# Gated linear attention with a SoLU layer: weight pieces fetched apart, part of a conversion moved between two groups of masks, constants made on GpSimd, and a finish moved ahead

## The chip, the cores and the metric

The kernel runs on one core of one Trainium2 chip. The metric is the device time in microseconds (us) of one execution, as the median of three runs. A core has five engines with a queue of instructions each: TensorE (PE; its weight loads are shown as PEld), VectorE (DVE), ScalarE (ACT), GpSimd (POOL) and SyncE (SP), which here issues most of the transfers. They wait for one another by semaphores. Sixteen DMA engines move data between the device memory and the core's own memory.

## The reference

Four batches, eight heads, 768 tokens, 48 values a head. A state per head decays by a gate and takes up the product of key and value; the query reads it. The result, as 3072 rows of 384, goes through a layer with the activation x*softmax(x), a layer norm with gains, and a second matrix.

```python
for t in range(S):
    state = alpha[:, :, t, :, None] * state + np.einsum('bhd,bhe->bhde', k[:, :, t], v[:, :, t])
    y[:, :, t] = np.einsum('bhd,bhde->bhe', q[:, :, t], state)
# x: y as (B*S, H*D)
h = x @ w_in                      # w_in 384 x 1024, float64
solu = h * softmax(h)
ln = (solu - mean(solu)) / np.sqrt(var(solu) + 1e-06) * g_ln
out = ln @ w_out                  # w_out 1024 x 384, float64
```

## The kernel before

The tokens are cut into six groups of 128 per batch. For each group the kernel turns the gates, keys and queries so that the values of a head lie on the partitions, runs scans over the tokens (`scan_back`, `scan_on`), multiplies keys and queries with them, makes the scores of all pairs of tokens in two halves of the heads (`scores`), cuts them to the triangle (`masked`, by a product with a mask of ones and zeros), and reads values and state (`read_values`, `read_state`) into `y`. The four batches' `y` are then the input of `up` for this group: eight pieces of 128 columns, each with an exponential on ScalarE, a product on VectorE and a square on ScalarE. `down` multiplies with the second matrix, one "chunk" of 128 tokens at a time, and `finish` scales the chunk and stores it. The attention of group g+1 is woven into `up` of group g by tables of steps.

The head of the kernel, with cuts:

```python
load_first(alpha, an, 0)
nc.scalar.dma_start(out=ident, in_=inline(np.eye(P), "ident_c"))
nc.scalar.dma_start(out=mask, in_=inline(np.triu(np.ones((P, P))), "mask_c"))
# ... parity and gains, also from the scalar queue
load_first(k, kn, 0)
load_first(q, qn, 0)
# ... memsets on GpSimd: vt, unit, aT, hT, seed, state
load_v_first(0)
fetch(0, 3, 2)          # weight pieces 0 and 1 together into slots 3 and 4
fetch(2, 1, 2)          # pieces 2 and 3
nc.vector.memset(ones, 1.0)
# ...
warm(16)                # 16 matmuls of ones, nothing uses them
turned(an, ends_of(an), t)      # transposes on TensorE, with ident
# ... scans, keys, queries
scores(0, 0)
scores(0, 1, t)
read_begin()
for b in (2, 3):        # two of the four first masks go over ScalarE and GpSimd
    s = sT[:, b, 0:NP]
    nc.scalar.copy(out=s, in_=masks[0][b])
    nc.gpsimd.tensor_tensor(out=s, in0=s, in1=mask[:, None, :].to_broadcast([P, NP, P]), op=ALU.mult)
masked(0, range(2))
masked(1)
bits(0)
read_values(0)
gains()
keys_back(0)
in_range(0)
bits(1)
in_range(1)
for f in range(FC):     # up of group 0
    up_mm(0, f)
    # ...
```

The weights are float64 and the kernel computes in float32. `fetch` brings the raw words, and `bits` makes float32 of them in five VectorE operations; it can be called by halves. A `fetch` of n pieces brings each of its (two or three) parts in one transfer for all n.

```python
def bits(i, part=None):
    lo, hi = raws[i][:, :, :, 0], raws[i][:, :, :, 1]
    if part != 1:
        # ... two operations: top
    if part != 0:
        # ... three operations: low, low, and the sum into w_in or w_out
```

The second stretch that the change touches, the start of `up` of group 1, with the attention of group 2:

```python
for i in range(3):
    scan_back(2, i)
keys_T(2)
keys(2)                 # products on GpSimd
load(k, kn, 3)
scan_on(2, 2)
scan_on(2, 0)
read_values(1)
alpha_over(2)
load(alpha, an, 3)
down(3, 1, slice(3, HF))
# ...
first = dict(
    head={3: "keys_back", 5: "masked0", 6: "masked1"},
    behind={0: "states v", 1: "lasts on1", 2: "firsts", 3: "apart", 5: "decay", 7: "alpha back"},
    tail={4: "scores0", 5: "scores1", 6: "begin read0 read1"},
    middle={7: "read2 read3 values"},
)
# ... for g in range(1, G + 1):
    after = B - 1 if g == 1 else None
    for s in range(FC):
        at("head", s)
        up(g, s)
        if after is not None:
            finish(after)
            after = None
        at("behind", s)
        # ... running sums, down, tail
```

`lasts` and `firsts` turn the queries on VectorE and multiply them on GpSimd, `apart` multiplies them with the parity on ScalarE, `states` adds to the state. `finish` of a chunk is four small VectorE operations (the last of them 128x384), one power on GpSimd (`r`), one scaling on ScalarE (`o_sb`) and a store.

Of the kernel before, what the change touches and what calls it, by code (L numbers as in the profile page):

```python
# [14 lines left out]
ALU = mybir.AluOpType  # L15
AX = mybir.AxisListType
P = 128
# [15 lines left out]
def fast_path(ctx, tc, q, k, v, alpha, moe_w_in, moe_w_out, moe_g_ln, out):  # L33
# [12 lines left out]
    nc = tc.nc  # L46
    B, H, S, D = q.shape
# [30 lines left out]
    ident = const.tile([P, P], FP, name="ident")  # L78
    mask = const.tile([P, P], FP, name="mask")
    ones = const.tile([P, P], FP, name="ones")  # L80
# [148 lines left out]
    def scan_on(g, i):  # L229
        part = slice(NP * i, NP * i + NP)  # L230
        if i == 2:

            nc.vector.reciprocal(out=seed[:, :, 0:1], in_=h4[:, :, 1:2])
            nc.scalar.copy(out=fend[:, g], in_=h4[:, :, 1])
        scan(aT[:, part], aT[:, part], seed[:, part], False)
# [53 lines left out]
    def masked(half, batches=range(B)):  # L289
        a = masks[half]  # L290
        for b in batches:
            nc.vector.tensor_tensor(  # L292
                out=sT[:, b, half * NP : half * NP + NP], in0=a[b], in1=mask[:, None, :].to_broadcast([P, NP, P]),
                op=ALU.mult,
            )
# [198 lines left out]
    def down(n, half, part=slice(0, HF)):  # L494
        g, b = divmod(n, B)
        d = st[n]
        if half == 0 and part.start == 0:
            d["o"] = ps_o.tile([P, 512], FP, tag="o", name="o")
        for f in range(half * HF + part.start, half * HF + part.stop):
            nc.tensor.matmul(  # L500
                d["o"][:, 0 : DM + 1], lhsT=u_of(g, f)[:, b * P : b * P + P], rhs=w_out[:, f], start=(f == 0),
                stop=(f == FC - 1), skip_group_check=True,
            )
# [7 lines left out]
    def finish(n):  # L511
        g, b = divmod(n, B)
        d = st[n]
        s, o = sums[:, n], d["o"][:, 0:DM]
        t0 = b * S + g * P
        if g == G - 1:
            o_sb = work.tile([P, DM], FP, name="o_sb")
            r = gr[g]["r"][:, b : b + 1]
            nc.scalar.activation(out=o_sb, in_=o, func=AF.Copy, scale=r)
            nc.scalar.dma_start(out=out[t0 : t0 + P, :], in_=o_sb)  # L520
            d.clear()
            return
        nc.vector.tensor_copy(out=s[:, 0:1], in_=d["o"][:, DM : DM + 1])
        t = small.tile([P, 1], FP, name="t")
        nc.vector.scalar_tensor_tensor(
            out=t, in0=s[:, 0:1], scalar=-1.0 / DFF, in1=s[:, 0:1], op0=ALU.mult, op1=ALU.mult
        )
        nc.vector.tensor_tensor(out=s[:, 3:4], in0=t, in1=gr[g]["s"][:, b : b + 1], op=ALU.add)  # L528
        if g == 0:

            if not d.get("moved"):
                o = work.tile([P, DM + 1], FP, name="o_mean")[:, 0:DM]
            nc.vector.scalar_tensor_tensor(
                out=o, in0=mean_sb, scalar=s[:, 0:1], in1=d["o"][:, 0:DM], op0=ALU.mult, op1=ALU.add
            )
        r = small.tile([P, 1], FP, name="r")
        nc.gpsimd.tensor_tensor(out=r, in0=s[:, 3:4], in1=mhalf, op=ALU.pow)  # L537
        o_sb = work.tile([P, DM], FP, name="o_sb")
        nc.scalar.activation(out=o_sb, in_=o, func=AF.Copy, scale=r)  # L539
        nc.sync.dma_start(out=out[t0 : t0 + P, :], in_=o_sb)  # L540
        d.clear()
# [16 lines left out]
    def fetch(i, slot, n=1):  # L558

        kind, f = pieces[i]  # L560
        w = n * F // (2 if kind else KC)
        raw = room[:, 1536 * slot : 1536 * (slot + n)].bitcast(U32).rearrange("p (c f w) -> p c f w", f=w, w=2)
        if kind:
            parts = [(slice(0, P), c, moe_w_out[(f + c) * P : (f + c + 1) * P, :]) for c in range(2)]
        else:
            parts = [(slice(0, P), c, moe_w_in[c * P : (c + 1) * P, f * P : f * P + w]) for c in range(KC)]
        for rows, c, src in parts:
            if float64:
                nc.sync.dma_start(out=raw[rows, c].rearrange("p f w -> p (f w)"), in_=src.bitcast(U32))
            else:  # L570
                dst = w_out[rows, f + c, 0:DM] if kind else w_in[rows, c, f * P : f * P + w]
                nc.sync.dma_start(out=dst, in_=src)
        for m in range(n):
            raws[i + m] = raw[:, :, w // n * m : w // n * (m + 1)]
# [14 lines left out]
    def bits(i, part=None):  # L589
        if not float64:  # L590
            return
        lo, hi = raws[i][:, :, :, 0], raws[i][:, :, :, 1]
        if part != 1:
            made[i] = [
                two.tile([P, F], FP, tag="two", name=x).rearrange("p (c f) -> p c f", c=hi.shape[1])
                for x in ("top", "low")
            ]
            top = made[i][0].bitcast(U32)
            nc.vector.tensor_scalar(
                out=top, in0=hi, scalar1=3, scalar2=0x3FFFFFF8, op0=ALU.logical_shift_left, op1=ALU.bitwise_and  # L600
            )
            nc.vector.scalar_tensor_tensor(
                out=top, in0=hi, scalar=0xC0000000, in1=top, op0=ALU.bitwise_and, op1=ALU.bitwise_or
            )
        if part != 0:
            top, low = made.pop(i)
            nc.vector.tensor_scalar(
                out=low.bitcast(U32), in0=top.bitcast(U32), scalar1=0xFF800000, scalar2=None, op0=ALU.bitwise_and
            )
            nc.vector.scalar_tensor_tensor(out=low, in0=lo, scalar=2.0**-52, in1=low, op0=ALU.mult, op1=ALU.mult)  # L610
            nc.vector.tensor_tensor(out=place(i), in0=low, in1=top, op=ALU.add)
# [34 lines left out]
    def inline(x, name):  # L646
        return nc.inline_tensor(np.ascontiguousarray(x, np.float32), name=name).ap()

    load_first(alpha, an, 0)
    nc.scalar.dma_start(out=ident, in_=inline(np.eye(P), "ident_c"))  # L650
    nc.scalar.dma_start(out=mask, in_=inline(np.triu(np.ones((P, P))), "mask_c"))
    odd = np.arange(P) // E1 % 2
    nc.scalar.dma_start(out=parity, in_=inline(np.stack([1 - odd, odd], 1), "parity_c"))
    nc.scalar.dma_start(out=g_rows, in_=moe_g_ln.rearrange("(c p) -> c p", p=P))
# [7 lines left out]
    nc.gpsimd.memset(seed, 0.0)  # L662
    nc.gpsimd.memset(state, 0.0)
    load_v_first(0)
    fetch(0, 3, 2)
    fetch(2, 1, 2)
    nc.vector.memset(ones, 1.0)
    nc.vector.memset(small_ones, 1.0 / 32)
    nc.vector.memset(mhalf, -0.5)
    nc.vector.memset(mone, -1.0)  # L670
# [26 lines left out]
    for i in (2, 0, 1):  # L697
        if i == 1:
# [3 lines left out]
            out=qe if i == 2 else qv[:, part], in0=t[i], in1=aT[:, part, 1:SW], op=ALU.mult  # L702
# [7 lines left out]
    for b in (2, 3):  # L710
        s = sT[:, b, 0:NP]
        nc.scalar.copy(out=s, in_=masks[0][b])
        nc.gpsimd.tensor_tensor(out=s, in0=s, in1=mask[:, None, :].to_broadcast([P, NP, P]), op=ALU.mult)
    masked(0, range(2))
    masked(1)
    bits(0)
    read_values(0)
    gains()
    keys_back(0)
# [94 lines left out]
    for i in range(3):  # L814
# [2 lines left out]
    keys(2)  # L817
    load(k, kn, 3)
    scan_on(2, 2)
    scan_on(2, 0)  # L820
    read_values(1)
    alpha_over(2)
    load(alpha, an, 3)
    down(3, 1, slice(3, HF))

# [5 lines left out]
    )  # L833
    first = dict(
        head={3: "keys_back", 5: "masked0", 6: "masked1"},
        behind={0: "states v", 1: "lasts on1", 2: "firsts", 3: "apart", 5: "decay", 7: "alpha back"},
        tail={4: "scores0", 5: "scores1", 6: "begin read0 read1"},
        middle={7: "read2 read3 values"},
    )
# [51 lines left out]
    for g in range(1, G + 1):  # L891
        rise, att = g < G, g + 1 < G
        plan = first if g == 1 else usual

        def at(where, s):
            for what in plan[where].get(s, "").split() if att else ():
                attend(g + 1, what)

        after = B - 1 if g == 1 else None
        if not rise:  # L900
            break
        for s in range(FC):
            at("head", s)
            if rise:
# [4 lines that stand above are left out]
            if s == 0 and g > 1:  # L909
                token_sums(g - 1)  # L910
            at("behind", s)
            for f in centres.get(s, ()) if g == 1 else ():
                centre(f)
            if rise and s:
                running(g, s)
            at("middle", s)
            if rise and s == FC - 1:
                todo.append((g * B, 0))
            step = todo.pop(0)
            if step:  # L920
                n, half = step
                down(n, half)
                if half:
                    after = n
            at("tail", s)
        if after is not None:
            finish(after)
        todo = [(n, half) for n in range(g * B, g * B + B) for half in range(2)][1:]
# [30 lines left out]
    else:  # L959
# [9 lines left out]
        out=bad, in0=all_ok[0:1, 0:1], scalar1=float(P * ends[-1]), scalar2=None, op0=ALU.is_lt  # L969
# [451 lines left out]
```

## Time and profile before

| what | value |
|---|---|
| median of 3 runs | 380.51 us (380.48 to 380.82) |
| span of the profiled execution | 378.7 us |
| mean granted TensorE clock | 0.997 |
| VectorE in 94 to 119 us | busy nearly without a gap |
| weight pieces 0 and 1 | first use by VectorE at 25.28 us, after 0.72 us of waiting |
| first matmul of `up` of group 0 | 29.97 us |
| first matmul of `up` of group 1 | 102.58 us |
| loads of identity and mask | 64 KB each, 1.9 and 3.4 us from issue to landing |

The profile is one execution. Its page gives busy times of the engines, the span in 40 slices (a digit is the busy share in tenths), the DMA queues, a chain of work that ended last, and groups of instructions. The trace behind it can be asked for the timeline of an engine: start, duration, engine, line of the kernel, operation, output and inputs, count; in square brackets the idle time of the engine ahead of it and what ended it. A line that stands for several instructions is merged. A duration on TensorE ends where its model puts the end. TensorE executes a float32 matmul as two passes, which the counts show (32 records for `warm(16)`). "issue" is time in which an engine waited for nothing that the profile shows.

### The profile page before, as it was taken

The page shows a single profiled execution, that of the slowest core. Times are in us where ns is not written, and L with a number is a line of the kernel's source. Part 1 is how long each engine was busy: PE and PEld are TensorE (multiplying, and loading weights), DVE is VectorE, ACT ScalarE, POOL GpSimd, SP SyncE. Part 2 cuts the span into 40 slices and gives each one's busy share as a digit, 9 for nine tenths or more (in the row PEclk, how much of TensorE's full clock was granted, in tenths as well). Part 3 has the DMA queues.
Part 4 walks back from the last instruction along what each step waited for, and adds up shares of the span by engine and source line. Part 5 has one row for each costly group of instructions (what it writes and reads, how often), then busy time and mean ns, then how long its engine had stood idle before and what let it go on. Part 6 is the DMA issues. An engine that isn't in the chain of part 4 may idle for free.

```text
span 378.7 us, 10523 instructions
## 1 busy us (share of the span) xinstructions
PE 365.5 (97%) x4659; PEld 219.2 (58%) x4659; DVE 244.1 (64%) x379; ACT 146.8 (39%) x263; POOL 129.4 (34%) x134
## 2 busy tenths in 40 slices
PE   8779999999998999999999999999999999999995
PEld 8675355567654565555575555675556675555552
DVE  1988879988997876874665874665865411455410
ACT  3628774493455152224451224451233131233111
POOL 5040000042148970662630671630672420333210
PEclk9999999999999999999999999999999999999998
DMA  9983989304097001960002940002300000000011
GB/s 187 190 309 100 223 273 159 85 0 128 24 215 141 4 5 31 182 144 21 23 25 39 205 112 23 23 24 46 62 0 23 24 23 2 22 21 21 23 44 49
DMA packets 65526, 30.78 MB, mean 81 GB/s; under 512 B 47032, under 2 KB 63680, under 8 KB 65472
## 3 DMA queue, kind: packets, MB, share of 16 engines
q1 hardware_dynamic: 64448, 29.10, 34.5%
q10 hardware_dynamic: 1024, 0.92, 0.7%
q8 instruction: 38, 0.62, 0.7%
q14 instruction: 16, 0.13, 0.1%
HBM read 25.30 MB, written 4.72 MB: 79 GB/s over the span
## 4 chain that ended last, share of the span: by engine, by line
PE 74%; DVE 11%; DMA 4%; ACT 4%; SPq 3%; issue 2%; ACTq 0%
PE o L500 30%; PE h L389 26%; PE y L315 8%; PE a L281 5%; DMA an<-in_alpha_dram 3%; SPq L153 2%; DVE hT L222 2%; DMA qn<-in_q_dram 2%; DVE sT L292 1%; PE kv L364 1%; PE tp L300 1%; DVE aT L197 1%; DVE room L404 1%; SPq L141 1%; ACT sq L214 1%
## 5 line engine op out<-in xcount | busy, mean ns | idle before, releaser
L500 PE MATMUL o<-w_out,room 128*128 128x385 f32 x384 | 133.8, 491 | 0.0
L389 PE MATMUL h<-x,w_in 128*128 128x512 f32 x288 | 132.4, 599 | 0.5 <-DVE room L404 0.4
L500 PEld LDWEIGHTS o<-w_out,room 128*128 128x128 f32 x384 | 71.2, 190 | 55.8 <-issue 13.1
L389 PEld LDWEIGHTS h<-x,w_in 128*128 128x128 f32 x288 | 52.8, 189 | 59.7 <-issue 48.2
L404 DVE TENSOR_TENSOR room<-h,e 128x512 f32<-128x512 f32 x40 | 27.6, 690 | 81.2 <-ACT e L403 81.1
L403 ACT ACTIVATE e<-h 128x512 f32<-128x512 f32 x40 | 23.9, 597 | 107.3 <-PE h L389 107.3
L420 POOL TENSOR_TENSOR p<-p,e 128x512 f32<-128x512 f32 x30 | 41.8, 1394 | 15.7 <-ACT e L403 15.6
L537 POOL TENSOR_TENSOR r<-sums,mhalf 128x1 f32<-128x1 f32 x20 | 14.9, 747 | 80.5 <-DVE sums L528 80.4
L405 ACT ACTIVATE u<-room 128x512 f32<-128x512 f32 x40 | 25.2, 631 | 38.4 <-DVE room L404 38.4
L292 DVE TENSOR_TENSOR sT<-a,mask 128x512 f32<-128x512 f32 x42 | 26.1, 682 | 8.3 <-PE a L281 8.2
L263 POOL TENSOR_TENSOR state<-state,hT 128x192 f32<-128x192 f32 x20 | 11.3, 582 | 53.4 <-DVE hT L222 53.4
L243 POOL TENSOR_TENSOR kT<-kT,hT 128x1024 f32<-128x1024 f32 (+1 forms) x8 | 14.2, 1796 | 42.2 <-DVE kT L197 42.2
L222 DVE TENSOR_TENSOR_SCAN hT<-aT,unit 128x516 f32<-128x516 f32 x18 | 23.2, 1355 | 7.5 <-ACT aT L683 7.4
L420 DVE TENSOR_TENSOR p<-p,u 128x512 f32<-128x512 f32 x30 | 22.8, 759 | 6.5 <-ACT u L405 6.5
L222 DVE TENSOR_TENSOR_SCAN aT<-aT,seed 128x516 f32<-128x516 f32 x18 | 26.6, 1508 | 0.2
L281 PEld LDWEIGHTS a<-qv,kT 32*128 32x128 f32 x704 | 21.8, 186 | 8.5 <-issue 2.4
L281 PE MATMUL a<-qv,kT 32*128 32x128 f32 x704 | 24.5, 278 | 1.7 <-POOL qv L254 0.8
L315 PE MATMUL y<-sT,vn 128*32 128x128 f32 x768 | 23.6, 274 | 2.6 <-issue 2.1
L315 PEld LDWEIGHTS y<-sT,vn 128*32 128x32 f32 x768 | 20.9, 110 | 4.8 <-issue 3.8
L214 ACT ACTIVATE sq<-an,mone 128x1536 uint8<-128x1536 f32 x12 | 18.9, 1574 | 0.2
L315 PE MATMUL y<-qv,state 32*32 32x128 f32 x960 | 16.7, 277 | 0.1
L539 ACT ACTIVATE o_sb<-o,r 128x384 f32<-128x384 f32 x16 | 9.3, 581 | 18.8 <-POOL r L537 18.8
(146 smaller groups left out, 373.0 us busy)
## 6 DMA issues: line engine op xcount, KB each, us to landing
an<-in_alpha_dram SPq DMA_DIRECT2D x20, 192.0 KB, 4.2
vn<-in_v_dram SPq DMA_DIRECT2D x10, 384.0 KB, 6.3
out_dram<-o_sb SPq DMA_DIRECT2D x20, 192.0 KB, 1.9
room<-in_moe_w_in_dram SPq DMA_DIRECT2D x6, 512.0 KB, 8.4
room<-in_moe_w_out_dram SPq DMA_DIRECT2D x8, 384.0 KB, 4.1
kn<-in_k_dram SPq DMA_DIRECT2D x16, 192.0 KB, 4.8
qn<-in_q_dram SPq DMA_DIRECT2D x16, 192.0 KB, 3.6
kn<-in_k_dram SPq DMA_DIRECT2D x4, 384.0 KB, 5.9
```

The lines of the kernel that those rows point to most:

```text
L214: nc.scalar.activation(out=sq, in_=x, func=AF.Relu, scale=sign, bias=mone, accum_out=over[:, g, i : i + 1])
L222: nc.vector.tensor_tensor_scan(out=o, data0=a, data1=s, initial=1.0, op0=ALU.mult, op1=ALU.add)
L281: nc.tensor.matmul(a[b][:, i], lhsT=kT[quarter(b), kb], rhs=qv[quarter(b), qb], start=kb == h, stop=kb != h, tile_position=(32 * b, 0), sk ...
L292: nc.vector.tensor_tensor(out=sT[:, b, half * NP : half * NP + NP], in0=a[b], in1=mask[:, None, :].to_broadcast([P, NP, P]), op=ALU.mult,)
L315: nc.tensor.matmul(y_bank(b)[quarter(r), a], lhsT=lhsT, rhs=rhs, start=(b, r) not in begun, stop=stop, tile_position=(row, 32 * r), skip_g ...
L389: nc.tensor.matmul(h, lhsT=w_in[:, a, f * P : (f + 1) * P], rhs=d["x"][:, a].rearrange("p b t -> p (b t)"), start=(a == 0), stop=(a == KC ...
L403: nc.scalar.activation(out=e, in_=h, func=AF.Exp)
L404: nc.vector.tensor_tensor(out=u, in0=h, in1=e, op=ALU.mult)
L405: nc.scalar.activation(out=u2, in_=u, func=AF.Square)
L420: eng.tensor_tensor(out=p, in0=d[0][i] if f == 1 else p, in1=d[f][i], op=ALU.add)
L500: nc.tensor.matmul(d["o"][:, 0 : DM + 1], lhsT=u_of(g, f)[:, b * P : b * P + P], rhs=w_out[:, f], start=(f == 0), stop=(f == FC - 1), skip ...
L537: nc.gpsimd.tensor_tensor(out=r, in0=s[:, 3:4], in1=mhalf, op=ALU.pow)
```

## The change

Four things change. Identity and mask are no longer loaded but made on GpSimd from a tile of ones, which is now set first. The first two weight pieces come by separate transfers, so that the first can be used before the second is there. The first two of the five operations that convert piece 0 stand between the masks of the first and of the second scores, so that VectorE has something to do while the second scores are made. And at the start of `up` of group 1 the finish of the fourth chunk stands ahead of the loop, no longer behind the first piece, while one scan moves from ahead of the loop to behind its second piece, and the turning of the queries' ends by one step.

```diff
     load_first(alpha, an, 0)
-    nc.scalar.dma_start(out=ident, in_=inline(np.eye(P), "ident_c"))
-    nc.scalar.dma_start(out=mask, in_=inline(np.triu(np.ones((P, P))), "mask_c"))
+    nc.vector.memset(ones, 1.0)
+    for x, op in ((ident, ALU.is_equal), (mask, ALU.is_ge)):
+        nc.gpsimd.affine_select(
+            out=x, in_=ones, pattern=[[1, P]], compare_op=op, fill=0.0, base=0, channel_multiplier=-1
+        )
@@
-    fetch(0, 3, 2)
+    fetch(0, 3)
+    fetch(1, 4)
     fetch(2, 1, 2)
-    nc.vector.memset(ones, 1.0)
@@
     masked(0, range(2))
+    bits(0, 0)
     masked(1)
-    bits(0)
+    bits(0, 1)
     read_values(0)
@@
     scan_on(2, 2)
-    scan_on(2, 0)
     read_values(1)
     alpha_over(2)
     load(alpha, an, 3)
     down(3, 1, slice(3, HF))
+    finish(3)
@@ first = dict(
-        behind={0: "states v", 1: "lasts on1", 2: "firsts", 3: "apart", 5: "decay", 7: "alpha back"},
+        behind={0: "states v", 1: "on0 on1", 2: "lasts firsts", 3: "apart", 5: "decay", 7: "alpha back"},
@@
-        after = B - 1 if g == 1 else None
+        after = None
```

## The prediction

> **What bounds the kernel now.** I read the page first, then the chain that ended last for the two stretches that the diff edits, then the timeline of each engine there, then the DMA queues by window. The page says that TensorE carries the kernel:
>
> ```profile
> PE 365.5 (97%) x4659; PEld 219.2 (58%) x4659; DVE 244.1 (64%) x379; ACT 146.8 (39%) x263; POOL 129.4 (34%) x134
> ...
> PE   8779999999998999999999999999999999999995
> ```
>
> Of 378.7 us, 13.2 are without a matmul. Only slices 1 to 3 (to 28.4 us) are visibly thin. So a change can gain only where TensorE waits: about 4.3 us in 8 to 30 us (by stages 4.54 busy of 6.70, 5.29 of 5.50, 7.89 of 9.80), and small pieces later. Everything that only moves other engines under a full TensorE is worth nothing.
>
> The head, from the chain in order of time (start, us, what):
>
> ```profile
> 8.09 6.59 DMA qn<-in_q_dram
> ...
> 16.71 0.69 DVE qe L701
> ...
> 22.10 0.68 DVE sT L292
> 22.78 0.04 issue
> 22.82 1.07 PE y L315 x23
> 23.89 1.49 issue
> 25.38 3.04 PE y L315 x101
> 28.42 0.15 PE tp_g L622
> 28.57 1.46 PE tp L300 x12
> 30.03 2.75 PE h L389 x6
> ```
>
> The reader is to see that the queries' arrival starts the path, that four masks by VectorE release the value reads `y`, and that these stand still for 1.49 us on nothing that a semaphore explains. From 30.03 the up-projection `h` runs almost without a gap.
>
> The second stretch, from the timelines of VectorE, ScalarE, GpSimd and TensorE (start, us, engine, line):
>
> ```profile
> 103.74 4.48 DVE L222 TENSOR_TENSOR_SCAN aT<-aT,seed 128x516 f32<-128x516 f32 x2
> 108.14 0.66 DVE L404 TENSOR_TENSOR room<-h,e 128x512 f32<-128x512 f32 x1
> ...
> 105.70 0.58 ACT L403 ACTIVATE e<-h 128x512 f32<-128x512 f32 x1
> ...
> 102.87 4.26 POOL L243 TENSOR_TENSOR kT<-kT,hT 128x1024 f32<-128x1024 f32 x2 [8.18 <-DVE kT L197]
> ...
> 119.57 0.50 PE L281 MATMUL a<-qv,kT 32*128 32x128 f32 x8 [0.76 <-POOL qv L254]
> 120.58 2.01 PE L281 MATMUL a<-qv,kT 32*128 32x128 f32 x56 [0.51 <-ACT qv L247]
> ```
>
> Here VectorE is dense from 94 to 119 us; TensorE pays 0.76 + 0.51 us before the scores of the third group. A second score group at 125.29 takes 3.44 us where its like takes 2.07, another 1.4 us behind the masks.
>
> [...] in 0 to 6 us queue q10 (identity, mask, parity, gains) took 9.3% of the 16 engines, 0.56 us, while q1 brought alpha and the keys. [...] three scans at 97.18 take 3.58 us (1.19 each), the two beside GpSimd's key products 2.24 each. [...] The trace has 38 packets of 0.62 MB, 16.3 KB each; one of them at 22.0 to 22.5 us, three us ahead of the end of the 1.49 us stop. That this packet is the awaited one is my reading, not shown.
>
> **The change part by part.**
>
> Identity and mask. Two 64 KB loads go. By their share of q10 (256 of 448 packets but nearly all the bytes) I put them at 0.45 us of all engines. Alpha can gain little: the warm matmuls end at 6.42 and the first transposes begin at 6.35 anyway, so only the second half of alpha counts, about 0.15. The queries land at 14.68 and should land 0.45 earlier. VectorE's scan ends at 16.45 and then waits 0.27 for the query transposes; 0.27 plus alpha's 0.15 gives 0.4 to 0.45. So the first masks begin near 19.8 instead of 20.24 and end near 21.1. GpSimd pays two selects of 128x128; from its memset of 128x516 at 0.53 I estimate 0.2 to 0.4 each. Its memsets then end near 6.2 instead of 5.46; the first of them that is needed (`unit`) is due at 8.45. Free.
>
> First two pieces apart. Both now wait for one 1.5 MB group, which lands at 25.28. The single transfers behind it: the second of 512 KB, issued at 17.08, landed after 4.9 us, at 22.0; the third near 25.06. Piece 0 alone is 768 KB, 1.5 such transfers in landed order; by 22.0 two of them were there. So I put piece 0 at 21.2 to 21.7, less 0.4: about 21.3 at the latest that matters.
>
> Half a conversion between the masks. The two `top` operations are 0.95 + 0.96 = 1.93 us with their gap. Before, VectorE idled 0.55 ahead of the second masks and 0.72 ahead of the conversion; both are filled. With the start at 21.3: `top` to 23.25, second masks 23.25 to 25.75 instead of 22.08 to 24.56. The first `y` goes at 23.95 instead of 22.82. The reads need 128 passes: 101 took 3.04, so 3.85 in all, and they end at 27.8 instead of 28.42, if the 1.49 us stop lies over before TensorE gets there. I expect that: if the packet of 22.25 leads by three us, it is ready at 25 or before, and TensorE reaches the 27th pass only at 24.8. The rest of the conversion (0.56 + 0.97 + 0.96) ends at 28.3, ahead of the `h` at 29.4. Sum of the head: **-0.6 us**. The 0.9 us that VectorE is ahead afterwards lies under a full TensorE; the gap of 0.36 at 42.54 hangs on ScalarE's exponentials, which move with `h`. The earlier loads into slot 3 (before at 33.76) feed nothing that waits.
>
> The finish and the scan. After: scan of the ends, finish of the fourth chunk, then `h*e` of the first piece, state sums, `h*e` of the second, and only then the two other scans, `lasts`, `firsts`. On VectorE this is the same work. But the order of the engines shows something that the diff does not say: ScalarE now has the chunk's output scaling ahead of the first exponential, and that scaling waits for GpSimd's `r`, which stands behind the key products (end 107.13). So `r` 107.15 to 107.7, scaling to 108.3, exponential to 108.85 (before 105.70 to 106.28), `h*e` at 108.9 instead of 108.14: +0.75. The gain elsewhere: one scan no longer runs beside the key products (about 1 us), and 0.45 of ScalarE's wait for `r` at 109.92 goes. Carried on with the durations of before: second `h*e` 110.7 (before 111.05), scans to 114.2, running sum to 114.9, third `h*e` 114.9 (115.24), `lasts` to 116.55, `firsts` to 118.55 (117.96), sum, fourth `h*e` 119.2 (118.56), parity products on ScalarE 120.5 (119.82), scores' second part at 121.2 (120.58). Sum of this part: **+0.5 us**, as both score groups hang on it.
>
> Together -0.6 + 0.5 = -0.1: from the median of 380.51 to **380.4 us**.
>
> **The rivals.** First, the head gives nothing: piece 0 lands at 22 or later, since the page gives 8.4 us median from issue to landing for these transfers. Then VectorE waits with the second masks behind it, `y` ends at 28.4 or 28.8, and the total is 380.9 to 381.3. For it: the third transfer needed three us more than the second. Against it: the second's 22.0.
>
> Second, the instruction stop stays at its old time or even comes later. With its end at 25.38, `y` ends at 28.42 as before, the head is zero, the total 381.0. For it: it ends within 0.1 us of the weight pieces' landing, and these bytes are the same. Against it: two like stops (0.40 at 99.55 and 0.26 at 139.66) follow instruction packets (97.0 to 97.5, 136.5 to 137.0) by 2.3 to 2.9 us, away from any weight piece.
>
> Third, the second stretch gains rather than loses: the three scans' contention falls by more than the late exponential costs, `firsts` ends near 117.3, the scores start 0.6 earlier, total 379.3. For it: VectorE is the dense engine there. Against it: the wait on `r` is in ScalarE's order.
>
> **Range and chances.** The two terms are each about 0.6 in size with an error as large: head -0.9 to +0.3, second stretch -0.6 to +0.9. Added as independent errors this is about 1 us either way, so 379.3 to 381.6. Two per cent is 7.6 us, more than all of TensorE's waits in both stretches; a loss of that size would need a stall of which I see no trace. So faster by over 2%: 0.01, within 2%: 0.98, slower: 0.01.
>
> **What would show it.** In the chain after: first `h` at 29.4 (right), at 30.0 or later (head wrong). The idle time ahead of the first `top`: none or 0.2 us (piece 0 in time) or near a microsecond (first rival). A stop inside `y`: gone or moved. First `h*e` of the second group about 0.75 late against its `h`, with ScalarE waiting for `r` ahead of the exponential; scores of the third group later by half a microsecond against the first `h` of the second group. The prediction is wrong if the selects delay the transposes beyond 6.4, or if a term is over 1 us off.

## The result and the profile after

The changed kernel takes 383.33 us (median of 4, 383.24 to 384.13) against 380.5 us (380.0 to 380.82, 4 runs) of the kernel before: ratio 1.008, 95% interval 1.0063 to 1.0098. It is slower by 2.8 us where 380.4 was predicted, and outside the predicted range of 379.3 to 381.6, though within 2%.

The page of the changed kernel: span, busy times, slices of TensorE, and the shares of the chain that ended last.

```profile
span 381.5 us, 10529 instructions
...
PE 366.5 (96%) x4659; PEld 220.3 (58%) x4659; DVE 244.5 (64%) x379; ACT 146.9 (39%) x263; POOL 129.7 (34%) x136
...
PE   8769999999898999999999999999999999999995
...
PE 69%; DVE 15%; ACT 5%; SPq 4%; issue 3%; DMA 1%; POOL 0%; DVEq 0%; ACTq 0%
```

TensorE is busy 1.0 us longer than before (366.5 against 365.5) and idle 15.0 us where it was idle 13.2. As many matmuls run; the warming ones alone took 6.70 us here and 5.38 before, which is more than the longer busy time (why that isn't the cause of the loss: below). The slices show little; the chain shows where the time is. Here it is for the head of the changed kernel (start, us, what):

```profile
17.66 4.77 DMA room<-in_moe_w_in_dram
...
22.56 0.89 DVE top L599
...
23.47 1.90 DVE top L602
...
25.37 0.61 DVE sT L292
...
26.03 3.69 PE y L315 x124
...
29.87 0.60 PE tp L300 x4
```

Before, the chain came to `y` from the scores. Now it comes from a weight transfer issued at 17.66: the conversion that was meant to fill a gap has become what the value reads wait for. The timelines show the same stretch from both sides. VectorE of the changed kernel:

```profile
21.00 1.29 DVE L292 TENSOR_TENSOR sT<-a,mask 128x512 f32<-128x512 f32 x2 [0.30 <-PE a L281]
22.56 0.88 DVE L599 TENSOR_SCALAR top<-room 128x768 uint32<-128x768 uint32 x1 [0.27 <-DMA room<-in_moe_w_in_dram]
23.47 1.90 DVE L602 SCALAR_TENSOR_TENSOR top<-room,top 128x768 uint32<-128x768 uint32 x1
25.29 1.28 DVE L292 TENSOR_TENSOR sT<-a_h,mask 128x512 f32<-128x512 f32 x2
```

GpSimd beside it (it multiplies two tiles of the first scores with the mask):

```profile
21.75 2.81 POOL L716 TENSOR_TENSOR sT<-sT,mask 128x512 f32<-128x512 f32 x2 [0.47 <-ACT sT L715]
```

Before, the same masks and the same two operations on VectorE, and GpSimd's two products:

```profile
22.08 1.29 DVE L292 TENSOR_TENSOR sT<-a_h,mask 128x512 f32<-128x512 f32 x2 [0.55 <-PE a_o L281]
...
25.28 0.95 DVE L599 TENSOR_SCALAR top<-room 128x768 uint32<-128x768 uint32 x1 [0.72 <-DMA room<-in_moe_w_in_dram]
26.27 0.96 DVE L602 SCALAR_TENSOR_TENSOR top<-room,top 128x768 uint32<-128x768 uint32 x1
...
21.10 2.51 POOL L713 TENSOR_TENSOR sT<-sT,mask 128x512 f32<-128x512 f32 x2
```

And TensorE of the changed kernel:

```profile
22.74 0.41 PE L315 MATMUL y<-sT,vn 128*32 128x128 f32 x4
26.03 3.69 PE L315 MATMUL y<-sT,vn 128*32 128x128 f32 x124 [2.87 <-DVE sT L292]
...
31.16 2.74 PE L389 MATMUL h<-x,w_in 128*128 128x512 f32 x6
```

Two things can be read off. The second conversion operation takes 1.90 us where it took 0.96, and from 22.56 to 24.56 GpSimd works beside the pair; before, GpSimd was done with its products at 23.61 when the pair began at 25.28. And TensorE, which began the first four value reads at 22.74, then stands for 2.87 us until the second masks are done; the stop of 1.49 us on "issue" that the kernel before has after its 27th value read no longer shows. The first `h` starts at 31.16 instead of 29.97.

Followed on down TensorE's timeline, the lag of the changed kernel is +1.2 us at the first `h`, +1.5 at the value reads of the second stretch (97.19 there, 98.68 here), +1.7 at the first `h` of group 1 (102.58, 104.28), +2.1 at the scores' second part (120.58, 122.69) and +2.8 at the end. Two stops on "issue" contribute to the later part: one inside the reads near 100 us, 0.40 long before and 0.95 now, and one of 0.35 at 199.8 that the kernel before doesn't show.

### The profile page after: what moved, and what is told of

It is laid out like the page before. It is cut to its first block, busy times and chain, and to the rows that moved or that the text cites. A ratio compares the mean times of both kernels' runs of the same rounds, so it can differ in the third digit from the quotient of the medians.

```text
span 381.5 us, 10529 instructions
## 1 busy us (share of the span) xinstructions
PE 366.5 (96%) x4659; PEld 220.3 (58%) x4659; DVE 244.5 (64%) x379; ACT 146.9 (39%) x263; POOL 129.7 (34%) x136
## 3 DMA queue, kind: packets, MB, share of 16 engines
HBM read 25.17 MB, written 4.72 MB: 78 GB/s over the span
## 4 chain that ended last, share of the span: by engine, by line
PE 69%; DVE 15%; ACT 5%; SPq 4%; issue 3%; DMA 1%; POOL 0%; DVEq 0%; ACTq 0%
PE o L500 30%; PE h L389 24%; PE y L315 8%; PE a L281 5%; SPq L153 2%; DVE room L404 2%; DVE hT L222 2%; DVE top L602 2%; DVE sT L292 1%; ACT sq L586 1%; DMA room<-in_moe_w_in_dram 1%; SPq L189 1%; DVE aT L197 1%; DVE aT L222 1%; PE kv L364 1%
## 5 line engine op out<-in xcount | busy, mean ns | idle before, releaser
L405 ACT ACTIVATE u<-room 128x512 f32<-128x512 f32 x40 | 25.2, 631 | 36.8 <-DVE room L404 36.8
```

The source lines that it names most:

```text
L405: nc.scalar.activation(out=u2, in_=u, func=AF.Square)
```

## The experiments

The theory that this suggests: the half conversion between the masks costs the time, because VectorE and GpSimd get into each other's way there (`top` 0.88 + 1.90 us instead of 1.93 with the gap for the pair), and because its data land at 22.4. Rivals: the constants made on GpSimd, which delay the warming matmuls (32 of them take 6.70 us here, 5.38 before) and with them all that follows; the second stretch; and the fetching apart by itself. All medians of this section are beside runs of the kernel before on the same chip: 380.51 us for the first four, 380.33 for `e5` to `e8`, 380.44 for `e9` to `e12`.

**`e1_ident`: the constants alone.**

```
-    nc.scalar.dma_start(out=ident, in_=inline(np.eye(P), "ident_c"))
-    nc.scalar.dma_start(out=mask, in_=inline(np.triu(np.ones((P, P))), "mask_c"))
+    nc.vector.memset(ones, 1.0)
+    for x, op in ((ident, ALU.is_equal), (mask, ALU.is_ge)):
+        nc.gpsimd.affine_select(out=x, in_=ones, pattern=[[1, P]], compare_op=op, ...)
```

> The kernel before with identity and mask made on GpSimd, nothing else changed. Theory (the loss sits in the conversion between the masks and in the second stretch): within 0.5 us of before, 380.0 to 381.0, first h of group 0 between 29.7 and 30.6 us, whatever the warm matmuls do. Rival (the slow phase of the warm matmuls, 6.70 us instead of 5.38, comes from this part and pushes everything behind it): warm matmuls 6.7 us again, first transposes near 7.7, first h near 31.2, total 381.6 to 382.

Measured: 380.26 us (379.66 to 383.03, 13 runs), ratio 1.0 (0.9986 to 1.0014). The constants are neither a gain nor the loss. In the profile, an execution of 382.44 us, the first `h` stands at 31.81, outside the expected range; its reads ran at a granted clock of 0.50 from 26 to 28 us, which the end of this document shows.

**`e2_apart`: the two pieces fetched apart alone.**

```
-    fetch(0, 3, 2)
+    fetch(0, 3)
+    fetch(1, 4)
```

> The kernel before with the first two weight pieces fetched by separate transfers, nothing else changed. Theory: the 0.72 us wait of VectorE ahead of the first conversion goes or shrinks, but the reads of the values end as before, so 380.3 to 380.8. Rival (smaller transfers are slower and delay all that is queued behind them): 381 or more, piece 1 landing later than 25.3.

Measured: 379.74 us (379.2 to 380.47, 13 runs), ratio 0.998 (0.9972 to 0.9988): a small gain, below the expected 380.3 to 380.8. VectorE of this kernel, where the conversion stands behind all masks and GpSimd's products are over:

```profile
24.75 0.55 DVE L599 TENSOR_SCALAR top<-room 128x768 uint32<-128x768 uint32 x1
25.33 0.96 DVE L602 SCALAR_TENSOR_TENSOR top<-room,top 128x768 uint32<-128x768 uint32 x1
```

No wait stands in front of them, where the kernel before waited 0.72 us for both pieces. The first `top` is also shorter, 0.55 us instead of 0.95, with GpSimd silent in both kernels. That comes with the fetch: with GpSimd silent, one half of a jointly fetched pair takes 0.94 to 0.97 us in every profile, a piece fetched alone 0.55 or 0.56. Pieces 2 and 3, still a pair here, take 0.94 us each, and 0.55 in `e12_four`, which fetches them apart.

**`e3_half`: apart, and half a conversion between the masks.**

```
     masked(0, range(2))
+    bits(0, 0)
     masked(1)
-    bits(0)
+    bits(0, 1)
```

> The kernel before with pieces apart and with half a conversion between the masks. Theory: as in the changed kernel, the first piece lands after the first masks are done, the second top operation is stretched to about 1.9 us by GpSimd's mask products, the second masks begin near 25 us instead of 22.08, and the value reads end near 29.5 instead of 28.42: total 381.4 to 381.9. Rival (warm matmuls are the cause): 380.2 to 380.6, since the warm matmuls of the kernel before take 5.4 us.

Measured: 382.99 us (382.26 to 383.65, 5 runs), ratio 1.0071 (1.0058 to 1.0084), a microsecond above the expected range. Beside `e2_apart` that is 3.25 us for two instructions moved. VectorE:

```profile
20.78 1.29 DVE L292 TENSOR_TENSOR sT<-a,mask 128x512 f32<-128x512 f32 x2 [0.30 <-PE a L281]
22.07 1.15 DVE L599 TENSOR_SCALAR top<-room 128x768 uint32<-128x768 uint32 x1
23.25 1.90 DVE L602 SCALAR_TENSOR_TENSOR top<-room,top 128x768 uint32<-128x768 uint32 x1
25.07 1.27 DVE L292 TENSOR_TENSOR sT<-a_h,mask 128x512 f32<-128x512 f32 x2
```

In this execution piece 0 was there (no wait ahead of the first `top`), and still the pair takes from 22.07 to 25.15, 3.08 us where 1.54 were needed in `e2_apart` (24.75 to 26.29). So the loss doesn't need a wait for the piece. TensorE again waits 2.87 us for the masks.

**`e5_half_nogp`: the same, without GpSimd's two mask products.** This kernel leaves out part of the work: for the two score tiles that GpSimd masks, ScalarE writes zeros in place of the scores, so the first four heads of two batches of group 0 get nothing from within their own chunk.

```
-        nc.scalar.copy(out=s, in_=masks[0][b])
-        nc.gpsimd.tensor_tensor(out=s, in0=s, in1=mask[...].to_broadcast([P, NP, P]), op=ALU.mult)
+        nc.scalar.mul(out=s, in_=masks[0][b], mul=0.0)
```

> Pieces apart and half a conversion between the masks, as in the run of that part alone (382.99), but the two first masks that go over ScalarE and GpSimd are left out: ScalarE writes zeros there, so GpSimd does nothing beside the conversion; the first four heads of two batches are left out of the output of group 0. Theory (GpSimd's products stretch the two top operations from 1.5 to 3 us): top operations 0.55 to 0.95 and 0.96 us, second masks begin near 23.6 instead of 25.07, value reads end near 28 instead of 29.5, total 380.8 to 381.8. Rival (it is the place of the conversion or the late piece, not GpSimd): top still above 2.5 us in all or waiting for the piece, total 382.5 or more.

Measured: 381.01 us (380.11 to 383.31, 21 runs), ratio 1.0033 (1.002 to 1.0046), against 1.0071 of `e3_half`; the intervals lie apart. VectorE:

```profile
20.10 1.29 DVE L292 TENSOR_TENSOR sT<-a,mask 128x512 f32<-128x512 f32 x2 [0.30 <-PE a L281]
22.46 0.56 DVE L599 TENSOR_SCALAR top<-room 128x768 uint32<-128x768 uint32 x1 [1.07 <-DMA room<-in_moe_w_in_dram]
23.05 0.96 DVE L602 SCALAR_TENSOR_TENSOR top<-room,top 128x768 uint32<-128x768 uint32 x1
23.93 1.28 DVE L292 TENSOR_TENSOR sT<-a_h,mask 128x512 f32<-128x512 f32 x2
```

This is the reading on which most rests: same instructions, same place in the order, the weight transfers of the head still under way, only GpSimd silent, and the pair has its undisturbed 0.56 + 0.96 us back. It also shows the other half of the fault: with the masks earlier, piece 0 is 1.07 us late. So even with GpSimd silent the kernel is no faster than the kernel before. (The value reads end at 30.03, not near 28 as expected: they too were slow in this execution, 5.36 us for 124 where `e3_half` takes 3.69.)

The second `top` has two inputs (0.96 us alone, 1.90 beside the products), the first has one (0.55 or 0.56 alone, 0.88 and 1.15 beside them). Both lost time; by what means the two engines hinder each other, no run shows. The prediction had read a like loss from the scans (1.19 us each alone, 2.24 beside GpSimd's key products) and didn't look for it here.

The ends of the operations show more than their lengths. GpSimd's second product ends at 24.56 in the changed kernel, 24.34 in `e3_half` and 23.80 in `e9_half_busy` (below), and the second `top` ends 0.81 us after it in each: 25.37, 25.15 and 24.61. It is as if most of its 0.96 us of work had waited for the product's end. In `e9_half_busy` GpSimd's first product ended 0.06 us after the first `top` had begun; that `top` took 0.56 us, and it was GpSimd's second product that became longer, 1.67 us instead of 1.29.

**`e10_nohalf`: the changed kernel without the half conversion.** The test from the other end.

```
-    bits(0, 0)
     masked(1)
-    bits(0, 1)
+    bits(0)
```

> The changed kernel with the conversion of piece 0 whole behind both groups of masks again; identity and mask on GpSimd, pieces apart, finish and scans as in the change. Theory (the half conversion carries the whole loss, and the parts add up): 380.5 - 0.25 - 0.77 + 0.6 = 380.1, between 379.7 and 380.7. Rival (the parts work on one another, the late start of the second stretch or the warm matmuls matter): 381.3 or more.

Measured: 380.71 us (380.62 to 382.03, 14 runs), ratio 1.0008 (0.9991 to 1.0025): all the rest of the change together is about nothing, at the upper edge of the expected range, and giving the conversion its old place takes 2.6 us off 383.33.

**`e4_second`, `e7_finish`, `e8_scans`: the second stretch, whole and in its two parts.** `e4_second` is the kernel before with all edits of the second stretch; `e7_finish` has the first diff alone, `e8_scans` the second alone.

```
     down(3, 1, slice(3, HF))
+    finish(3)
@@
-        after = B - 1 if g == 1 else None
+        after = None
```

```
     scan_on(2, 2)
-    scan_on(2, 0)
@@
-        behind={0: "states v", 1: "lasts on1", 2: "firsts", ...},
+        behind={0: "states v", 1: "on0 on1", 2: "lasts firsts", ...},
```

> The kernel before with the finish of the fourth chunk ahead of the loop and the scan and the turning of the queries' ends moved behind. Theory: plus 0.5 to 0.7 us (381.0 to 381.2), ScalarE's scaling of the chunk ahead of its first exponential of group 1, first product h*e about 0.8 later against its h. Rival (the difference seen in the changed kernel only grew out of the shifted head): 380.3 to 380.7.

> The kernel before with only the finish of the fourth chunk moved ahead of the loop, the scans as before. Theory (the loss of the second stretch comes from ScalarE's scaling, which waits for GpSimd's power behind the key products and holds up the first exponential): plus 0.3 to 1.0 us, 380.8 to 381.5. Rival (the loss comes from the moved scan and turning): 380.3 to 380.7.

> The kernel before with only the scan and the turning of the queries' ends moved behind, the finish as before. Theory: VectorE reaches the first product h*e about 1 us sooner, total 379.9 to 380.6. Rival (the loss comes from here): 380.9 to 381.3.

Measured: `e4_second` 381.1 us (380.63 to 384.39, 12 runs), ratio 1.0032 (1.0014 to 1.0051); `e7_finish` 382.12 us (381.3 to 383.81, 7 runs), ratio 1.0053 (1.0035 to 1.0072); `e8_scans` 380.58 us (379.83 to 382.99, 22 runs), ratio 1.0012 (1.0002 to 1.0022). The finish alone costs 1.8 us, more than expected. In its trace ScalarE holds the first exponential behind the output scaling, which waits for GpSimd's `r`:

```profile
108.61 0.61 ACT L539 ACTIVATE o_sb<-o_mean,r 128x384 f32<-128x384 f32 x1 [3.57 <-POOL r L537]
109.13 0.58 ACT L403 ACTIVATE e<-h 128x512 f32<-128x512 f32 x1
```

and TensorE waits in turn for the `h*e` that frees a tile:

```profile
110.48 2.84 PE L389 MATMUL h<-x,w_in 128*128 128x512 f32 x6 [1.56 <-DVE room L404]
```

With the scans moved as well, in `e4_second`, the same wait is short: one scan of some 2.2 us fewer stands on VectorE ahead of the sums from which `r` is made:

```profile
109.62 2.84 PE L389 MATMUL h<-x,w_in 128*128 128x512 f32 x6 [0.26 <-DVE room L404]
```

So the two edits belong together: the scan move, which by itself costs 0.25 us, pays back most of what the finish costs, and +0.6 us stays.

**`e6_warm12`: twelve warming matmuls instead of sixteen, with the pieces apart.** Made to test two things at once: whether the warming phase sets the start of the head, and whether the stops on "issue" belong to places in TensorE's instruction stream.

```
-    warm(16)
+    warm(12)
```

> Pieces apart (379.74) with 12 instead of 16 warm matmuls, which takes 8 matmul records and 8 weight loads out of TensorE's stream. Theory [...]: the stop inside the first value reads moves from after the 27th record to after the 35th, the one near 99.5 us from after the 63rd to after the 71st, time about the same, 379.3 to 380.2. Rival (they are waits on data or on the memory of results, fixed by what the instruction needs): same places, 27th and 63rd. If the slow phase of the warm matmuls gates the start, the shorter warming shows it: first transposes near 6.5, total unchanged or 0.3 less.

Measured: 380.92 us (380.18 to 382.68, 13 runs), ratio 1.0016 (1.0004 to 1.0029): over a microsecond more than `e2_apart`, not less, and above the expected range. The time gives the warming theory no support. Why it is longer isn't shown: in the two profiles the kernels are level at the first `h` of group 1 (102.27 and 102.25), and the 1.3 us between their spans come later. The trace answers the other question. TensorE of `e2_apart`:

```profile
23.09 1.07 PE L315 MATMUL y<-sT,vn 128*32 128x128 f32 x23 [0.42 <-DVE sT L292]
24.81 3.04 PE L315 MATMUL y<-sT,vn 128*32 128x128 f32 x101 [0.65 <-issue]
...
95.82 0.70 PE L315 MATMUL y<-qv,state 32*32 32x128 f32 x33 [0.42 <-issue]
...
96.92 1.95 PE L315 MATMUL y<-sT,vn 128*32 128x128 f32 x63
99.55 2.02 PE L315 MATMUL y<-sT,vn 128*32 128x128 f32 x65 [0.67 <-issue]
```

and of `e6_warm12`:

```profile
22.59 1.10 PE L315 MATMUL y<-sT,vn 128*32 128x128 f32 x31 [0.42 <-DVE sT L292]
25.26 2.82 PE L315 MATMUL y<-sT,vn 128*32 128x128 f32 x93 [1.57 <-issue]
...
96.76 2.17 PE L315 MATMUL y<-sT,vn 128*32 128x128 f32 x71
99.17 1.80 PE L315 MATMUL y<-sT,vn 128*32 128x128 f32 x57 [0.24 <-issue]
```

Eight matmul records fewer ahead, and both stops stand eight records later in the reads: 31 instead of 23, 71 instead of 63. In `e9_half_busy`, with 28 records more ahead, the second stop stands after the 36th read, 27 earlier. They move with the instruction count, not with the data and not with the time. And the two later stops of `e2_apart`, of 0.42 and 0.67 us, are 128 records apart (33, twice 16 in lines left out here, and 63). Across the executions profiled here in which no longer wait covers it, the first stop, beside the transfers of the head, is 0.34 to 1.82 us long. That a stop is a wait for one of the instruction packets (the page of the kernel before counts 38 of them in its queue q8, 0.62 MB) is the author's reading; no run shows it.

**`e9_half_busy`: `e3_half` with TensorE kept busy during the wait.** To see how much of the loss is a lower clock after the wait.

```
+    warm(14, ps_a, "a1")
     read_values(0)
```

> Pieces apart and half a conversion between the masks (382.99 with a profile at 382.26), plus 14 matmuls of ones on TensorE in its idle time of 2.9 us ahead of the value reads; nothing uses them. Theory ([...] 0.50 granted in two profiles, at 1.5 us a time): the slow executions go, median 382.0 to 382.5, span between lowest and highest under 1 us. Rival (the spread has another cause): median 382.7 or more, spread as before, 1.4 us or more.

Measured: 382.57 us (382.06 to 384.3, 6 runs), ratio 1.0061 (1.004 to 1.0083). This is inconclusive: the interval overlaps that of `e3_half`, and the added instructions shift the stops on "issue" as in `e6_warm12`. In its trace the extra matmuls fill 21.78 to 25.17, the reads run without a gap from 25.10, and a wait of 0.82 us, put down to a weight transfer, stands ahead of the transposition of the gains at 29.78. That transposition reads no weights, and the place is right behind 128 reads, where the next stop would stand by an estimate from the 128 records between the stops of `e2_apart`; which of the two it was isn't shown. The clocks say a little more: five of the six executions have a mean granted clock of 0.997 or more and take 382.06 to 382.89 us, in `e3_half` one of five (382.26). That would fit a TensorE that keeps its clock when busy, but on few executions. And the profiled one, at a mean granted clock of 0.999 and with its 128 reads in 3.86 us, still loses 1.6 us, so the clock isn't most of the loss.

**`e11_ident_apart` and `e12_four`: what is left that helps.** `e11_ident_apart` joins the edits of `e1_ident` and `e2_apart`; `e12_four` fetches all of the first four pieces apart.

```
-    fetch(0, 3, 2)
-    fetch(2, 1, 2)
+    fetch(0, 3)
+    fetch(1, 4)
+    fetch(2, 1)
+    fetch(3, 2)
```

> The kernel before with pieces apart and identity and mask on GpSimd. Theory: no less than pieces apart alone, 379.3 to 379.9. Rival (identity and mask cost something, as the wide spread of that run up to 383.0 hints): 380.3 or more.

> The kernel before with all first four pieces fetched apart. Theory ([...] stop of 0.65 instead of 1.49 us): as pieces apart alone or up to 0.3 less, 379.4 to 379.9, stop inside the first value reads at most 0.65. Rival (the gain comes from VectorE's earlier conversion alone, and more transfers only cost issue time): 380.0 or more.

Measured: `e11_ident_apart` 379.87 us (378.73 to 381.15, 22 runs), ratio 0.9985 (0.9975 to 0.9995); `e12_four` 380.04 us (379.16 to 381.2, 22 runs), ratio 0.9972 (0.9954 to 0.999). Both beat the two kernels, as does `e2_apart`, and their intervals overlap: 0.4 to 0.8 us by the medians are to be had from fetching apart, and neither the constants nor two more single fetches add anything that shows. In the profile of `e12_four` the stop inside the first reads is down to 0.34 us, as its theory wanted, but its time lies in the range of the rival. So it stays open whether fetching apart gains by a shorter stop or by the earlier conversion.

The warming rival: over the profiles the same 32 matmuls take 5.2 to 6.8 us. A slow start may cost something: the execution of `e12_four` with 6.76 us is the slowest of its kernel, 381.2 us. But it isn't the loss of 2.8 us. `e10_nohalf` keeps the constants and the whole start of the changed kernel and takes 380.71 us. And in `e5_half_nogp` and `e9_half_busy`, with 5.47 and 5.23 us of warming, the first `top` begins at 22.46 and 22.11, no earlier than in `e3_half` with 6.55 us (22.07), because there piece 0 is what it waits for.

**The ledger.** By medians against the kernel before on the same chip: constants -0.25, apart with half conversion +2.48, second stretch +0.59, together +2.82; the whole measures +2.83. By ratios it is 1 + 0 + 0.0071 + 0.0032 = 1.0103 against 1.008 (1.0063 to 1.0098), so that the parts add up to within a microsecond, and no better agreement is claimed.

## Why the prediction was wrong

**The half conversion between the masks: the step that failed.** It was to begin at 21.3 and to hold up the second masks until 23.25. It began at 22.56 and held them up until 25.29. So of the 2.0 us, 1.26 are a late start and the rest a longer pair of operations.

**Its cost.** "The two `top` operations are 0.95 + 0.96 = 1.93 us with their gap." Those are durations from a place where GpSimd was silent, of a piece that was part of a pair. Fetched alone, the two need only 0.55 + 0.96 (`e2_apart`). But in the new place GpSimd multiplies masks: the kernel before already showed it busy with them for 2.51 us from 21.10, and the prediction does not mention GpSimd in that window, though it had read from the scans what GpSimd's products cost VectorE there (1.19 us became 2.24). Measured: 0.88 + 1.90 us, and 0.56 + 0.96 when `e5_half_nogp` silences GpSimd.

**The landing.** "About 21.3 at the latest that matters." It landed at 22.43. Piece 0 is three parts of 256 KB. Its second and third, issued at 17.19 and 17.66, land after 3.7 and 4.8 us, at 20.9 and 22.4. In the other profiles with the pieces apart the third lands at 21.45 (`e11_ident_apart`) to 22.43 (`e2_apart`), always later than 21.3, though only 0.6 to 0.8 us behind the second. The estimate of 1.5 single transfers counted bytes at the pace of two landings; the three us between them (22.0 and, by the trace, 25.2) were used only as an argument for the first rival. That rival's event came true in the changed kernel and `e5_half_nogp`; its size, 380.9 to 381.3, was short by the contention. In the changed kernel the landing alone didn't set the start: its first masks, begun at 21.00 after a warming of 6.70 us, ended at 22.29, and 0.27 us of waiting for the piece were left.

**What follows from the two.** Predicted for the second masks 23.25, measured 25.29; first value read after the wait predicted 23.95, measured 26.03; end of the reads predicted 27.8, measured 29.7; first `h` predicted 29.4, measured 31.16. The head was to give -0.6 us and gives +1.2 in the profile. The other 1.6 us come later, with the second stretch and the stops in it and after it.

**The instruction stop.** "If the 1.49 us stop lies over before TensorE gets there": right in kind. `e6_warm12` shows that the stops move with the count of instructions (8 records later for 8 fewer ahead); that this one waited for the packet of 22.25 is not shown. In the changed kernel it no longer shows, and as the longer wait stands in its place, it could not become a gain. The second rival, that it stays, falls; its total, 381.0, would have been near the truth only by the way.

**The constants.** Two selects of 0.2 to 0.4 us were estimated; both took 0.29, and the 0.63 us ahead of the first are a wait for VectorE's sets, the tile of ones among them. GpSimd:

```profile
1.13 0.29 POOL L652 TENSOR_SCALAR_AFFINE_SELECT ident<-ones 128x128 f32<-128x128 f32 x1 [0.63 <-DVE w_out L674]
1.38 0.29 POOL L652 TENSOR_SCALAR_AFFINE_SELECT mask<-ones 128x128 f32<-128x128 f32 x1
```

They are done by 1.7 us and hold up nothing. The gain of 0.4 to 0.45 us that was put on the queries, an estimate from the two loads' share of queue q10, did not come: their transposition begins at 14.67 instead of 14.73, and in `e1_ident` at 14.58, the first masks there at 20.19 instead of 20.24. So taking two small loads off the DMA engines did not bring the queries forward by the time that these loads had taken.

**The second stretch: right in mechanism, and in size by the medians.** Predicted: the exponential waits for `r`, `h*e` 0.75 late, scores half a microsecond late, sum +0.5. In the changed kernel, ScalarE:

```profile
109.52 0.61 ACT L539 ACTIVATE o_sb<-o_mean,r 128x384 f32<-128x384 f32 x1 [2.14 <-POOL r L537]
110.04 0.58 ACT L403 ACTIVATE e<-h 128x512 f32<-128x512 f32 x1
```

and VectorE:

```profile
110.65 0.69 DVE L404 TENSOR_TENSOR room<-h,e 128x512 f32<-128x512 f32 x1 [1.27 <-ACT e L403]
```

From the first `h` of group 1 (104.28) to this `h*e` it is 6.37 us; before, 102.58 to 108.14, it was 5.56: 0.81 late. The scores' second part stands 18.41 us behind that `h` instead of 18.00. `e4_second` by itself costs 0.6 us by the medians, 1.2 by the ratio (0.5 to 1.9 by its interval). That the sum came out so near is in part luck: the finish alone costs 1.8 us, the scan move alone gains nothing, and the gain of about 1 us for a scan that no longer runs beside the key products is 0.3, as the three scans take 5.35 us in the changed kernel and 5.64 before. The third rival, a gain here, falls; the reason given against it, the wait on `r` in ScalarE's order, is the one that the trace shows.

**What stays open.** How the 3.25 us between `e3_half` and `e2_apart` divide. In the two profiles 1.64 us are there by the first `h` (30.94 against 29.30) and 1.86 at the reads near 100 us (101.41 against 99.55). An estimate from the executions with a mean granted clock of 0.997 or more alone, each against the kernel before on the same chip: `e2_apart` is at -0.8 us, `e5_half_nogp` at +0.4 (the median of eleven) and `e3_half` at +1.75 (one execution, the profiled). Then 1.2 us are the new place and the piece's landing, 1.3 the contention (which made the two operations 1.5 us longer), and 0.7 a lower clock in the other four executions of `e3_half`. As one execution carries it, the split is not shown. Why a stop lasts 0.3 us in one execution and 1.8 in another, and why the second and third part of piece 0 land 1.5 us apart in the changed kernel and 0.6 to 0.8 in the others, isn't settled either.

## What to carry to other kernels

Before an operation is moved into a gap of its own engine, look at every other engine in that window of the trace, GpSimd above all for VectorE (0.96 us became 1.90 beside it here), and take the operation's duration from a place with the same neighbours, or else measure it there. A gap in front of work that gates the busiest engine is no free room: whatever goes in has to be done, data landed and all, before the gap would have ended (here the second masks began at 25.29 instead of 22.08). Split a transfer whose first part is needed earlier; here that alone paid, with 0.8 us.

## What the runs showed of the hardware

**A lower clock after a short idle time.** In the profile of `e1_ident` TensorE's reads after a stop of 1.82 us take half as long again as elsewhere (3.04 for the same 101):

```profile
25.66 4.70 PE L315 MATMUL y<-sT,vn 128*32 128x128 f32 x101 [1.82 <-issue]
```

Busy time by stage of this kernel shows why (window, length, busy us of TensorE, its weight loads, VectorE, ScalarE, GpSimd with counts; then the granted TensorE clock, the DMA share and GB/s):

```profile
24.00:26.00 2.00, 0.34 (x12) 0.34 (x15) 0.99 (x2) 0.00 (x0) 0.00 (x0) 0.98 0.99 383
26.00:28.00 2.00, 2.00 (x46) 1.98 (x42) 1.93 (x3) 0.65 (x2) 0.00 (x0) 0.50 0.74 295
28.00:30.00 2.00, 2.00 (x57) 1.98 (x50) 1.93 (x3) 0.78 (x2) 0.00 (x0) 0.66 0.02 8
30.00:32.00 2.00, 2.00 (x26) 1.78 (x17) 1.46 (x4) 1.36 (x4) 0.00 (x0) 1.00 0.00 0
```

The granted clock is 0.50 from 26 to 28 us, 0.66 from 28 to 30 and 1.00 after that. In `e5_half_nogp` the reads were as slow after a wait of 2.41 us, 124 of them in 5.36 us instead of 3.69, in an execution with a mean granted clock of 0.995:

```profile
24.67 5.36 PE L315 MATMUL y<-sT,vn 128*32 128x128 f32 x124 [2.41 <-DVE sT L292]
```

In these two executions the slow reads came after 1.8 and 2.4 us without a matmul, with 23 and 4 reads just ahead of them. In `e3_half` and the changed kernel a wait of 2.87 us was followed by reads at full speed (124 in 3.69 us, in the changed kernel at a granted clock of 1.00 from 24 to 30 us), so it isn't the length alone; what decides it, no run shows. This costs such an execution some 1.7 us (4.70 - 3.04, 5.36 - 3.69), and the runs of `e5_half_nogp` fall into two groups: ten of its 21 executions have a mean granted clock of 0.994 to 0.996 and take 381.87 to 383.31 us, the eleven others have 0.998 or more and take 380.11 to 381.01. In the changed kernel the mean clock doesn't sort the times: 383.24 us with 0.997, 383.29 with 0.992.

**What VectorE and GpSimd cost each other, for single instructions.** Beside a GpSimd product of 128x512, VectorE's two-input operation over 128x768 took 1.90 us instead of 0.96, and ended 0.81 us behind the product. Its one-input operation took 0.88 and 1.15 instead of 0.55, and 0.56 where GpSimd's product came second. GpSimd lost less: its two products took 2.81 and 2.90 us instead of 2.51.

**A conversion of a piece that was fetched alone.** The same one-input operation over 128x768, without GpSimd, took 0.94 to 0.97 us on one half of a jointly fetched pair and 0.55 to 0.56 on a piece fetched alone.
